# Attention denominators of 86 units: a DMA transpose and a VectorE reduction in place of matmuls with ones, with the PV matmuls ten slots behind

## The chip, the cores and the metric

The kernel runs on one core of one Trainium2 chip. The metric is the device time of one execution in microseconds; the time before is the median of three runs. The engines of the core are TensorE (PE in the profile), VectorE (DVE), ScalarE (ACT), GpSimd (POOL) and SyncE (SP), which issues nearly all DMAs of this kernel from one in-order queue.

## What is computed

An attention block over a given cache of keys and values (32 heads, 2048 queries, 2048 keys, head size 128) runs on a layer-normed input and is multiplied by a gate, the silu of a small mixer and MLP block. All data is bf16. The reference, cut to the attention:

```python
q = (xn @ wq).reshape(B, Sq, H, Dh).transpose(0, 2, 1, 3)
scores = jnp.einsum("bhqd,bhkd->bhqk", q, k_cache) * (Dh ** -0.5)
p = softmax(scores, axis=-1)
o = jnp.einsum("bhqk,bhkd->bhqd", p, v_cache)
s = o.transpose(0, 2, 1, 3).reshape(B, Sq, H * Dh) @ wo
g = silu(B_ref(xn, B_w1, B_w2, B_w3, B_w4))
out = x + s * g
```

The softmax is computed without subtracting a maximum: the exponentials of all 2048 keys are used as they are, and the sum over the keys, the denominator of a query, is applied to o.

## The kernel before

A first stage of some 120 us normalises the input and computes most of the gate branch. Then comes attention, in 128 units. A unit is one head and 512 queries. Heads go in eight groups of four (HG = 4); in a group the order is by block of queries and then by head, and the last group is arranged a little differently. With one head's 2048 keys on 16 chunks of 128, a unit has 8 slots (SPU = 8) of two chunks each. The main loop counts slots: n = 8u + p for slot p of unit u.

The program order of each engine is fixed by hand: every instruction goes through `pin`, which keeps it in the order written, and each engine works through its own list in order. One slot of the main loop writes, as far as they fall due:

- `s_slot(u, p)`: two matmuls of keys with q into a score bank pair `ps_s` (two such pairs), and one exponential on ACT into half of a tile `pT` (four tiles, so 8 slots' worth).
- `pv_slot` of slot n - LAG, with LAG = 5: two matmuls of values with exponentials into `ps_o`. There are two `ps_o` banks, one for each unit under way.
- slots 0 and 1: `q_mm`, four matmuls in all for the q of the next unit; slot 2: `q_copy` on DVE.
- slots 4 and 5: `wo_slot`, four matmuls of the output projection for 128 queries of an earlier block, and in slot 6 its DVE addition into `sacc`.
- denominators: DVE adds the unit's four `pT` tiles (`add_first` at slot 4, `add_next` at slot 6, `add_last` at slot 0 of the next unit). `add_last` also folds the sum to one row of 512 queries by 128 partitions, `acc[:, 0, :]`. At slot 3 of the next unit `sums` turns these 128 partial sums per query into one with four matmuls: a 128x128 block of `acc` as weights, a column of ones as the moving operand. DVE takes the reciprocal of the 128x4 result, and a DMA stores it in DRAM (`dr`). At slot 4 `bcast` reads it back to all partitions (`rb`, 128x512 f32).
- `norm(u)` at slot 2 of unit u + 2: DVE multiplies `ps_o` with `rb` into `oT`. That frees the `ps_o` bank, and after the last head of a group it makes a block ready for the projection.
- loads: in 9 of 16 units SP issues two pieces of a key tile, as DMA transposes, and half of a value tile for the next group; other units load wq and wo. There are five key tiles and five value tiles (HG + 1).

The last 20 units have a different end: some units run more projection tiles, and two of them compute their denominators in another way, which the change leaves as it is.

What the change touches: `sums` (lines 318 to 328), `bcast` and `rb` (330 to 333), `norm` (335 to 341), the tiles named `tm` in `wo_post`, `late_mul` and `late_act`, the `pT` tiles (line 288), and the main loop, lines 632 to 668.

Of the kernel before, what the change touches and what calls it, by code (L numbers as in the profile page):

```python
# [9 lines left out]
ALU = mybir.AluOpType  # L10
FP32 = mybir.dt.float32
BF16 = mybir.dt.bfloat16
# [5 lines left out]
def kernel(  # L18
# [15 lines left out]
    nc = tc.nc  # L34
    P = nc.NUM_PARTITIONS
# [3 lines left out]
    Sq, D = x2d.shape  # L39
# [11 lines left out]
    HG = 4  # L51
    NG = H // HG

    SPU = KC // 2
    LAG = 5
# [6 lines left out]
    pin = tc.keep_in_program_order  # L62
# [25 lines left out]
    smp = ent(pool("smp", 4))  # L88
    tokp = ent(pool("tok", 4))
    drp = ent(pool("drp", 4, bass.MemoryType.DRAM))  # L90
# [31 lines left out]
    units += [(NG - 1, qt, hh) for qt in range(QT - 2) for hh in range(HG)]  # L122
    units += [(NG - 1, qt, HG - 1) for qt in LATE]
    NU = len(units)
    NS = NU * SPU
    kTs, vBs, wqs, wos, oTs, st = {}, {}, {}, {}, {}, {}
    todo = defaultdict(list)
# [135 lines left out]
    def q_mm(u, dcs, tag="xa"):  # L263
        g, qt, hh = units[u]
        if dcs[0] == 0:
            st[u] = dict(psq=psX.tile([P, 512], FP32, tag=tag, name="ps_q"))
        for dc in dcs:
            mm(st[u]["psq"][:], wqs[g * HG + hh][:, dc, :],
               xnT[:, dc, qt * 512:(qt + 1) * 512], dc == 0, dc == DC - 1)
# [9 lines left out]
    def s_slot(u, p):  # L279
        g, qt, hh = units[u]  # L280
        s = st[u]
        sps = psS.tile([P, 2, 512], FP32, name="ps_s")
        for j in range(2):
            kc = 2 * p + j
            kv = kTs[g * HG + hh].rearrange("d (i p j) -> d i j p", p=P, j=KJ)
            mm(sps[:, j, :], kv[:, kc // KJ, kc % KJ, :], s["qT"][:], True, True)
        if p % 2 == 0:
            s.setdefault("pT", []).append(pB.tile([P, 4, 512], BF16, tag="pT", bufs=4, name="pT"))
        jj = 2 * (p % 2)
        pin(nc.scalar.activation(  # L290
            out=s["pT"][-1][:, jj:jj + 2, :], in_=sps[:], func=ACT.Exp, scale=SCALE))
# [11 lines left out]
    def add_last(u):  # L303
        add_next(u, 3)
        a = st[u]["acc"]
        pin(nc.vector.tensor_tensor(out=a[:, 0:2, :], in0=a[:, 0:2, :], in1=a[:, 2:4, :], op=ALU.add))  # L306
        pin(nc.vector.tensor_tensor(out=a[:, 0, :], in0=a[:, 0, :], in1=a[:, 1, :], op=ALU.add))  # L307

    def pv_slot(u, p):
        g, qt, hh = units[u]  # L310
        s = st[u]
        if p == 0:
            s["o"] = psO.tile([P, 512], FP32, tag="ps_o", name="ps_o")
        pT = s["pT"][p // 2]
        for j in range(2):
            kc = 2 * p + j
            mm(s["o"][:], vBs[g * HG + hh][:, kc, :], pT[:, 2 * (p % 2) + j, :], kc == 0, kc == KC - 1)

    def sums(u):
# [7 lines left out]
        s["dr"] = drp.tile([P, 4], FP32, name="dr")  # L327
        pin(nc.sync.dma_start(out=s["dr"][:], in_=rc[:]))

    def bcast(u):  # L330
        st[u]["rb"] = pB.tile([P, 512], FP32, tag="rb", bufs=5, name="rb")
        pin(nc.sync.dma_start(
            out=st[u]["rb"][:], in_=st[u]["dr"][:].rearrange("p j -> (p j)").partition_broadcast(P)))

    def norm(u):
        g, qt, hh = units[u]
        s = st.pop(u)
        if hh == 0:
            oTs[(g, qt)] = pB.tile([P, HG, 512], BF16, tag="oT", bufs=2, name="oT")
        pin(nc.vector.tensor_tensor(  # L340
            out=oTs[(g, qt)][:, hh, :], in0=s["o"][:], in1=s["rb"][:], op=ALU.mult))

    wo_box = {}
    sacc = {}
# [28 lines left out]
    def wo_post(g, t, n, eng=nc.vector):  # L373
        ps = wo_box.pop(0)
        if g == 0:
            sacc[t] = pS.tile([P, D], FP32, tag="sacc", bufs=NT, name="sacc")
            pin(nc.vector.tensor_copy(out=sacc[t][:], in_=ps[:]))
            return
        sa, gl = sacc[t][:], xall[:, t, :]
        if t // 4 in LATE and g >= GY:  # L380
            tm = pB.tile([P, D], FP32, tag="rb", bufs=5, name="tm")
            pin(nc.vector.scalar_tensor_tensor(
                out=tm[:], in0=ps[:], scalar=0.5, in1=gl, op0=ALU.mult, op1=ALU.mult))
            pin(nc.vector.tensor_tensor(out=sa, in0=sa, in1=tm[:], op=ALU.add))
            return
        pin(nc.vector.tensor_tensor(out=sa, in0=ps[:], in1=sa, op=ALU.add))  # L386
        if t // 4 in LATE and g == GY - 1:
            k = n + SPU * (t - 4 * LATE[0]) + 1
            at(max(k - SPU, n + 1), lambda: fin_load(t))
            at(k, lambda: y_scale(t))  # L390
            at(k + SPU, lambda: y_add(t))
        if g < NG - 1:
            return
        xl = fin.pop(t)
        pin(nc.vector.scalar_tensor_tensor(  # L395
            out=gl, in0=sa, scalar=0.5, in1=gl, op0=ALU.mult, op1=ALU.mult))
        pin(eng.tensor_tensor(out=xl[:], in0=gl, in1=xl[:], op=ALU.add))  # L397
        pin(nc.sync.dma_start(out=out2d[t * P:(t + 1) * P, :], in_=xl[:]))
# [30 lines left out]

    def late_mul(u, ts, ps):  # L430
        t = 4 * units[u][1] + ts
        tm = pB.tile([P, D], FP32, tag="rb", bufs=5, name="tm")
        pin(nc.vector.scalar_tensor_tensor(
            out=tm[:], in0=ps, scalar=st[u]["rc"][:, ts:ts + 1], in1=xall[:, t, :],
            op0=ALU.mult, op1=ALU.mult))
        return tm

    def late_act(u, ts, ps):
        t = 4 * units[u][1] + ts
        tm = pB.tile([P, D], FP32, tag="rb", bufs=5, name="tm")  # L440
        pin(nc.scalar.activation(out=tm[:], in_=ps, func=ACT.Identity, scale=st[u]["rc"][:, ts:ts + 1]))
        pin(nc.gpsimd.tensor_tensor(out=tm[:], in0=tm[:], in1=xall[:, t, :], op=ALU.mult))
        return tm
# [132 lines left out]
    pS = None  # L576
# [30 lines left out]
            at(n + 4, lambda: gate_silu(t, th["a"]))  # L607

    wo_todo = deque()

    def norm_queue(u):
        norm(u)
# [6 lines left out]

    UA, UB = NU - 2, NU - 1  # L620

# [9 lines left out]

    for n in range(UB * SPU):
        u, p = divmod(n, SPU)
        extra = u >= NU - 10 and len(wo_todo) > 1
        s_slot(u, p)
        m = n - LAG
        if 0 <= m < NS:
            pv_slot(*divmod(m, SPU))
        if p in (0, 1) and 4 * HG - 1 <= u:
            q_mm(u + 1, (2 * p, 2 * p + 1))  # L640
        if p == 0 and 1 <= u:
            add_last(u - 1)
        if p == 0:
            twice = extra
        if twice and p < 3:
            wo_slot(p, n)
        if p == 2 and 4 * HG - 1 <= u:
            q_copy(u + 1)
        late = u > NU - 4 * HG
        if p == 2 + late and 2 <= u:  # L650
            norm_queue(u - 2)
        if p == 3 + late and 1 <= u:
            sums(u - 1)
        if p == 4 + late and 1 <= u:
            bcast(u - 1)
        if p in (4, 5, 6) and wo_todo:
            wo_slot(p - 4, n)
        if p == 4:
            add_first(u)
        if p == 6:  # L660
            add_next(u, 2)
        held_mm(n)
        for fn in todo.pop(n, ()):
            fn()
        if not held and not todo.get(n + 1) and pS is None and n >= 4 * SPU + 5:
            right.close()
            pS = right.enter_context(pool("pS", side="right", reuse_waits="tile"))
# [14 lines left out]
    for p in range(SPU + LAG):  # L682
        if p < SPU:
            s_slot(UB, p)
        pv_slot(*divmod(UB * SPU + p - LAG, SPU))
        if p == 0:
            add_next(UA, 3)
        if p == 1:
            late_ps(UA)
            late_sums(UA, [st[UA]["acc"][:, i, :] for i in range(4)], True, True)  # L690
            late_rc(UA)
        if p == 2:
            norm_queue(UB - 2)
            for t in range(1, 4):
                fin_load(4 * (QT - 3) + t)
        if p in (3, 6, 8, 10):
            wo_tile(nc.gpsimd if p < 10 else nc.vector)
        if p == 4:
            late_o(UA, nc.vector)
            add_first(UB)  # L700
        if p == 5:
            late_tile(UA, 0, bank(psX, "xa"))
        if p in (5, 7, 9):
            late_tile(UA, (p - 3) // 2, bank(psO, "ps_o"))
        if p == 9:
            late_ps(UB)
            late_sums(UB, [st[UB]["acc"][:, i, :] for i in range(4)], True, False)
        if p == 10:
            late_sums(UB, [st[UB]["pT"][2][:, i, :] for i in range(4)], False, False)
        if p == 11:  # L710
            late_sums(UB, [st[UB]["pT"][3][:, i, :] for i in range(2)], False, False)
        if p == 12:
            late_o(UB, nc.scalar)
            late_sums(UB, [st[UB]["pT"][3][:, i, :] for i in range(2, 4)], False, True)
# [44 lines left out]
```

## Time and profile before

| | us |
|---|---|
| median of 3 runs | 1277.88 (1277.77 to 1278.06) |
| the profiled execution, its time | 1278.11 |
| the profiled execution, its span | 1276.3 |
| mean granted TensorE clock | 0.997 |

The span runs from the first to the last instruction of the profiled execution. In a row of a timeline the columns are start, duration, engine, source line, operation, output and inputs with their shapes, and how many instructions are merged in the row; in brackets stands the engine's idle time before the row and what ended it. Matmuls are pipelined: the next starts before the one before has ended, so durations of PE rows overlap, and the distance between starts tells the pace. All matmuls are recorded at the line of one helper, 107, so they are told apart by their tiles. A row of a DMA on SP shows for how long the issue held SP's queue; the time to landing, from issue until the data is there, is told by the DMA view.

### The profile page before, as it was taken

The numbers are of one execution on the slowest core, as the hardware profiler recorded it, in microseconds if no ns is written. First come the engines' busy times: TensorE is split into PE (matmuls) and PEld (weight loads), VectorE is DVE, ScalarE is ACT, GpSimd is POOL, SyncE is SP. The second block draws the span as 40 slices with busy tenths as digits, with TensorE's granted clock in tenths as the row PEclk, the third lists the DMA queues.
The fourth block names the chain that finished last, engine by engine and source line by source line (L and its number), as shares of the span: only waits on it lengthen the run. The fifth ranks groups of instructions, "written<-read, shape, count | busy, mean of one in ns | idle before, by whom it ended". The sixth has DMA issues, their size and how long they took to land.

```text
span 1276.3 us, 16933 instructions
## 1 busy us (share of the span) xinstructions
PE 1253.6 (98%) x6199; PEld 611.3 (48%) x6324; DVE 957.4 (75%) x1333; ACT 1056.4 (83%) x1108; POOL 46.5 (4%) x100
## 2 busy tenths in 40 slices
PE   8999999999999999999999999999999999999996
PEld 4444444444444444444444444444444444444443
DVE  7621567777777777777777777777778888888887
ACT  5444789988888888888888888888888888888884
POOL 4320000000000000000000000000000000000003
PEclk9999999999999999999999999999999999999998
DMA  8282012453133412453234303442235314351122
GB/s 207 54 161 59 9 26 50 83 100 63 38 80 71 98 34 50 92 87 55 50 74 85 83 28 74 84 83 50 55 71 112 71 42 91 71 95 34 26 67 75
DMA packets 170323, 90.52 MB, mean 71 GB/s; under 512 B 122432, under 2 KB 153664, under 8 KB 170240
## 3 DMA queue, kind: packets, MB, share of 16 engines
q1 hardware_dynamic: 166880, 86.55, 33.2%
q0 software_dynamic: 672, 1.84, 0.7%
q10 hardware_dynamic: 2688, 1.05, 0.3%
q8 instruction: 49, 0.80, 0.3%
q14 instruction: 34, 0.28, 0.1%
HBM read 67.11 MB, written 2.36 MB: 54 GB/s over the span
## 4 chain that ended last, share of the span: by engine, by line
PE 95%; ACT 2%; DVE 2%; issue 1%; DMA 0%; DVEq 0%; ACTq 0%
PE ps_s L107 38%; PE ps_o L107 37%; PE ps_wo L107 8%; PE ps_q L107 8%; PE ps_m L107 2%; PE ps_sum L107 1%; ACT pT L290 1%; DVE acc L301 0%; PE ps_warm L107 0%; DMA kT<-in_A_k_cache_dram 0%; ACT xnT L198 0%; DVE xall L395 0%; DVE sacc L386 0%; ACT qT L276 0%; DVE acc L306 0%
## 5 line engine op out<-in xcount | busy, mean ns | idle before, releaser
L290 ACT ACTIVATE pT<-ps_s 128x1024 bf16<-128x1024 f32 x1024 | 991.5, 1026 | 136.4 <-PE ps_s L107 130.2
L107 PE MATMUL ps_o<-pT,vb 128*128 128x512 bf16 x2023 | 604.2, 379 | 3.1
L107 PE MATMUL ps_s<-qT,kT 128*128 128x512 bf16 x1989 | 597.4, 380 | 3.7 <-ACT pT L290 1.2
L301 DVE TENSOR_TENSOR acc<-acc,pT 128x2048 bf16<-128x2048 bf16 x254 | 310.2, 1221 | 60.5 <-ACT pT L290 58.8
L107 PEld LDWEIGHTS <-kT 128*128 128x128 bf16 x2048 | 223.2, 114 | 206.0 <-issue 6.3
L107 PEld LDWEIGHTS <-vb 128*128 128x128 bf16 x2048 | 199.7, 98 | 225.2 <-issue 0.2
L296 DVE TENSOR_TENSOR acc<-pT 128x2048 bf16<-128x2048 bf16 x128 | 157.0, 1227 | 49.0 <-ACT pT L290 49.0
L107 PE MATMUL ps_wo<-wo_h,oT 128*128 128x512 bf16 x500 | 149.2, 379 | 0.1
L107 PE MATMUL ps_q<-xnT,wq_h 128*128 128x512 bf16 x485 | 142.8, 379 | 0.1
L386 DVE TENSOR_TENSOR sacc<-ps_wo,sacc 128x512 f32<-128x512 f32 x96 | 66.4, 691 | 69.4 <-PE ps_wo L107 69.4
L306 DVE TENSOR_TENSOR acc<-acc 128x1024 bf16<-128x1024 bf16 x126 | 87.1, 692 | 4.3
L340 DVE TENSOR_TENSOR oT<-ps_o,rb 128x512 bf16<-128x512 f32 x126 | 85.8, 681 | 0.7 <-DMA rb<-dr 0.7
L107 PEld LDWEIGHTS <-wq_h 128*128 128x128 bf16 x512 | 49.9, 98 | 59.7 <-issue 0.3
L274 DVE CAST qT<-ps_q 128x512 bf16<-128x512 f32 x112 | 76.6, 684 | 0.0
L107 PEld LDWEIGHTS <-oT 128*128 128x128 bf16 x504 | 48.4, 98 | 56.7
L307 DVE TENSOR_TENSOR acc<-acc 128x512 bf16<-128x512 bf16 x126 | 53.6, 426 | 4.3
L107 PEld LDWEIGHTS <-acc 128*128 128x128 bf16 x536 | 37.8, 114 | 29.3 <-DVE acc L301 0.7
L107 PE MATMUL ps_s<-xn2T,w_sb 128*128 128x512 bf16 x219 | 48.6, 380 | 0.3
L241 ACT ACTIVATE h2T<-ps_s 128x1024 bf16<-128x1024 f32 x28 | 28.6, 1023 | 24.1 <-PE ps_s L107 24.1
L397 POOL TENSOR_TENSOR xl<-xall,xl 128x512 bf16<-128x512 bf16 x3 | 3.4, 1148 | 1182.9 <-ACT pT L290 1182.9
L107 PEld LDWEIGHTS <-w_sb 128*128 128x128 bf16 x304 | 29.6, 98 | 34.8 <-issue 1.9
L326 DVE RECIPROCAL rc<-ps_sum 128x4 f32<-128x4 f32 x126 | 23.0, 183 | 27.4 <-PE ps_sum L107 14.3
(64 smaller groups left out, 382.9 us busy)
## 6 DMA issues: line engine op xcount, KB each, us to landing
rb<-dr SPq DMA_DIRECT2D x126, 256.0 KB, 4.2
vb<-in_A_v_cache_dram SPq DMA_DIRECT2D x64, 256.0 KB, 4.4
wo_h<-in_A_wo_dram SPq DMA_DIRECT2D x32, 128.0 KB, 4.2
wq_h<-in_A_wq_dram SPq DMA_DIRECT2D x28, 128.0 KB, 4.2
w_sb<-in_B_w_dram SPq DMA_DIRECT2D x9, 256.0 KB, 5.8
kT<-in_A_k_cache_dram SPq DMA_TRANSPOSE x128, 4.4
xl<-in_A_x_dram SPq DMA_DIRECT2D x16, 128.0 KB, 3.7
dr<-rc SPq DMA_DIRECT2D x126, 2.0 KB, 1.4
```

What stands on the lines that cost most here:

```text
L107: pin(nc.tensor.matmul(out=out, lhsT=lhsT, rhs=rhs, start=start, stop=stop))
L241: pin(nc.scalar.activation(out=h2[c, f][:], in_=ps[:], func=ACT.Gelu_apprx_tanh))
L274: pin(nc.vector.tensor_copy(out=qT[:], in_=st[u].pop("psq")[:]))
L290: pin(nc.scalar.activation(out=s["pT"][-1][:, jj:jj + 2, :], in_=sps[:], func=ACT.Exp, scale=SCALE))
L296: pin(nc.vector.tensor_tensor(out=s["acc"][:], in0=s["pT"][0][:], in1=s["pT"][1][:], op=ALU.add))
L301: pin(nc.vector.tensor_tensor(out=a[:], in0=a[:], in1=st[u]["pT"][i][:], op=ALU.add))
L306: pin(nc.vector.tensor_tensor(out=a[:, 0:2, :], in0=a[:, 0:2, :], in1=a[:, 2:4, :], op=ALU.add))
L307: pin(nc.vector.tensor_tensor(out=a[:, 0, :], in0=a[:, 0, :], in1=a[:, 1, :], op=ALU.add))
L326: pin(nc.vector.reciprocal(out=rc[:], in_=ps[:]))
L340: pin(nc.vector.tensor_tensor(out=oTs[(g, qt)][:, hh, :], in0=s["o"][:], in1=s["rb"][:], op=ALU.mult))
L386: pin(nc.vector.tensor_tensor(out=sa, in0=ps[:], in1=sa, op=ALU.add))
L397: pin(eng.tensor_tensor(out=xl[:], in0=gl, in1=xl[:], op=ALU.add))
```

## The change

It has four parts.

1. For the 86 units u = 22 to 107 (`TURN`) the four matmuls of `sums` go. In their place `turn(u)`, at slot 3 of unit u + 1, issues a DMA transpose of `acc[:, 0, :]` (128 x 512 bf16, SBUF to SBUF) into a new tile `tT` of 128 x 4 x 128. `turned_sums(u)`, at slot 0 of unit u + 2, reduces `tT` on DVE along its last dimension to 128x4, takes the reciprocal and issues the store to `dr`; it stands ahead of `add_last(u + 1)` on DVE. `bcast(u)` follows at slot 1 of u + 2, and `norm(u)` at slot 7 of u + 2, both later than before. The transposed order of the queries is made up for in `norm`, which reads `rb` with a step of four.
2. PV goes from five slots behind the scores to ten: `pv_run` raises the lag by one at each of units 18 to 22 (no PV in the first slot of these) and lowers it by one at each of units 111 to 115 (two PV slots in the first slot). In the program as built, DVE's list has `norm`, then the reduction, the reciprocal and the three adds of `add_last`; SP's list has, for each such unit, store, broadcast, transpose, and then the loads of keys and values.
3. `pT` gets six tiles instead of four, `rb` two instead of five; `tm` gets four tiles of its own.
4. In the last 20 units a second projection tile is computed in a unit as soon as more than three are waiting; before this began only in the last ten.

```diff
+    TURN = range(5 * HG + 2, NU - 5 * HG)
+    PV0, PV1 = 4 * HG + 2, NU - 5 * HG + 3
...
-            s.setdefault("pT", []).append(pB.tile([P, 4, 512], BF16, tag="pT", bufs=4, name="pT"))
+            s.setdefault("pT", []).append(pB.tile([P, 4, 512], BF16, tag="pT", bufs=6, name="pT"))
...
+    def turn(u):
+        st[u]["tT"] = pS.tile([P, 4, P], BF16, tag="tT", bufs=2, name="tT")
+        pin(nc.sync.dma_start_transpose(out=st[u]["tT"][:], in_=st[u]["acc"][:, 0, :]))
+
+    def turned_sums(u):
+        s = st[u]
+        sm = smp.tile([P, 4], FP32, name="sm")
+        pin(nc.vector.tensor_reduce(out=sm[:], in_=s["tT"][:], axis=mybir.AxisListType.X, op=ALU.add))
+        rc = smp.tile([P, 4], FP32, name="rc")
+        pin(nc.vector.reciprocal(out=rc[:], in_=sm[:]))
+        s["dr"] = drp.tile([P, 4], FP32, name="dr")
+        pin(nc.sync.dma_start(out=s["dr"][:], in_=rc[:]))
...
-        st[u]["rb"] = pB.tile([P, 512], FP32, tag="rb", bufs=5, name="rb")
+        st[u]["rb"] = pB.tile([P, 512], FP32, tag="rb", bufs=2, name="rb")
...
-        pin(nc.vector.tensor_tensor(
-            out=oTs[(g, qt)][:, hh, :], in0=s["o"][:], in1=s["rb"][:], op=ALU.mult))
+        o, rb, to = s["o"][:], s["rb"][:], oTs[(g, qt)][:, hh, :]
+        if u in TURN:
+            o, to = (x.rearrange("k (j p) -> k j p", j=4) for x in (o, to))
+            rb = rb.rearrange("k (p j) -> k j p", j=4)
+        pin(nc.vector.tensor_tensor(out=to, in0=o, in1=rb, op=ALU.mult))
...
+    pv_at = [0]
+
+    def pv_run(n):
+        u = n // SPU
+        if u < PV0:
+            lag = LAG
+        elif u < PV0 + LAG:
+            lag = LAG + u - PV0 + 1
+        elif u < PV1:
+            lag = 2 * LAG
+        else:
+            lag = max(LAG, 2 * LAG - (u - PV1 + 1))
+        while pv_at[0] <= min(n - lag, NS - 1):
+            pv_slot(*divmod(pv_at[0], SPU))
+            pv_at[0] += 1
...
-        extra = u >= NU - 10 and len(wo_todo) > 1
+        extra = len(wo_todo) > (1 if u >= NU - 10 else 3) and u >= NU - 5 * HG
         s_slot(u, p)
-        m = n - LAG
-        if 0 <= m < NS:
-            pv_slot(*divmod(m, SPU))
+        pv_run(n)
         if p in (0, 1) and 4 * HG - 1 <= u:
             q_mm(u + 1, (2 * p, 2 * p + 1))
+        if p == 0 and u - 2 in TURN:
+            turned_sums(u - 2)
+        if p == 1 and u - 2 in TURN:
+            bcast(u - 2)
         if p == 0 and 1 <= u:
             add_last(u - 1)
+        if p == 3 and u - 1 in TURN:
+            turn(u - 1)
...
-        if p == 2 + late and 2 <= u:
+        if p == (7 if u - 2 in TURN else 2 + late) and 2 <= u:
             norm_queue(u - 2)
-        if p == 3 + late and 1 <= u:
+        if p == 3 + late and 1 <= u and u - 1 not in TURN:
             sums(u - 1)
-        if p == 4 + late and 1 <= u:
+        if p == 4 + late and 1 <= u and u - 1 not in TURN:
             bcast(u - 1)
```

More of the change, by code (lines that the diff above doesn't have):

```diff
@@ L380, in wo_post @@
         if t // 4 in LATE and g >= GY:
-            tm = pB.tile([P, D], FP32, tag="rb", bufs=5, name="tm")
+            tm = pS.tile([P, D], FP32, tag="tm", bufs=4, name="tm")
             pin(nc.vector.scalar_tensor_tensor(
@@ L431, in late_mul @@
         t = 4 * units[u][1] + ts
-        tm = pB.tile([P, D], FP32, tag="rb", bufs=5, name="tm")
+        tm = pS.tile([P, D], FP32, tag="tm", bufs=4, name="tm")
         pin(nc.vector.scalar_tensor_tensor(
@@ L439, in late_act @@
         t = 4 * units[u][1] + ts
-        tm = pB.tile([P, D], FP32, tag="rb", bufs=5, name="tm")
+        tm = pS.tile([P, D], FP32, tag="tm", bufs=4, name="tm")
         pin(nc.scalar.activation(out=tm[:], in_=ps, func=ACT.Identity, scale=st[u]["rc"][:, ts:ts + 1]))
@@ L684 @@
             s_slot(UB, p)
-        pv_slot(*divmod(UB * SPU + p - LAG, SPU))
+        pv_run(UB * SPU + p)
         if p == 0:
```

## The prediction

> **What bounds the kernel now.** I read the page first: the span, the engines' shares, and the engine that makes up the chain of waits.
>
> ```profile
> span 1276.3 us, 16933 instructions
> PE 1253.6 (98%) x6199; PEld 611.3 (48%) x6324; DVE 957.4 (75%) x1333; ACT 1056.4 (83%) x1108; POOL 46.5 (4%) x100
> PE 95%; ACT 2%; DVE 2%; issue 1%; DMA 0%; DVEq 0%; ACTq 0%
> ```
>
> TensorE (PE) is busy throughout and makes 95% of the chain. A busy PE need not be at its peak, so next comes the timeline of PE in one attention unit in mid-kernel.
>
> ```profile
> 704.43 0.60 PE L107 MATMUL ps_s<-qT,kT 128*128 128x512 bf16 x2
> 704.86 0.60 PE L107 MATMUL ps_o<-pT,vb 128*128 128x512 bf16 x2
> ...
> 707.02 0.59 PE L107 MATMUL ps_s<-qT,kT 128*128 128x512 bf16 x2
> ...
> 708.32 0.59 PE L107 MATMUL ps_o<-pT,vb 128*128 128x512 bf16 x2
> 708.75 0.27 PE L107 MATMUL ps_sum<-ones_t,acc 128*128 128x1 bf16 x4
> 708.88 0.60 PE L107 MATMUL ps_s<-qT,kT 128*128 128x512 bf16 x2
> ...
> 717.51 0.27 PE L107 MATMUL ps_sum<-ones_t,acc 128*128 128x1 bf16 x4
> 717.64 0.60 PE L107 MATMUL ps_s<-qT,kT 128*128 128x512 bf16 x2
> ```
>
> Starts are what count. Two 512-column matmuls take 704.86 - 704.43 = 0.43 us; the four summing matmuls hold the next score matmul back by 708.88 - 708.75 = 0.13 us, and again by 717.64 - 717.51 = 0.13. One period is 717.64 - 708.88 = 8.76 us: 40 matmuls in 717.51 - 708.88 = 8.63, plus the sums' 0.13. No gap stands anywhere, so in this stage each matmul taken away shortens the unit, if nothing else becomes late. Slot 0 starts at 704.43, slots 0, 1, 4 and 5 hold six matmuls (1.29 us), the others four (0.86).
>
> **What the change removes.** TURN is range(22, 108), so 86 of the 126 summed units lose four weight loads and four matmuls.
>
> 86 x 0.13 us = 11.2 us, all on the path.
>
> The Trainium skill, "TensorE: Matmul & The Clock Gate", section LDWEIGHTS, gives a weight load as columns / 1.2 ns, some 107 ns for 128. If each load stood in the open, four would be 0.43 us a unit and the saving an estimated 37 us; the 0.13 us between starts says that they do not, and the row decides.
>
> **What it adds on VectorE (DVE).** A unit's work there now, with ScalarE (ACT):
>
> ```profile
> 703.34 2.86 ACT L290 ACTIVATE pT<-ps_s 128x1024 bf16<-128x1024 f32 x3 [0.27 <-PE ps_s L107]
> 706.36 1.02 ACT L290 ACTIVATE pT<-ps_s 128x1024 bf16<-128x1024 f32 x1 [0.17 <-PE ps_s L107]
> 707.71 2.85 ACT L290 ACTIVATE pT<-ps_s 128x1024 bf16<-128x1024 f32 x3 [0.33 <-PE ps_s L107]
> ...
> 705.31 1.23 DVE L301 TENSOR_TENSOR acc<-acc,pT 128x2048 bf16<-128x2048 bf16 x1 [0.58 <-ACT pT L290]
> 706.57 0.69 DVE L306 TENSOR_TENSOR acc<-acc 128x1024 bf16<-128x1024 bf16 x1
> 707.29 0.42 DVE L307 TENSOR_TENSOR acc<-acc 128x512 bf16<-128x512 bf16 x1
> 707.64 0.68 DVE L274 CAST qT<-ps_q 128x512 bf16<-128x512 f32 x1
> 708.24 0.68 DVE L340 TENSOR_TENSOR oT<-ps_o,rb 128x512 bf16<-128x512 f32 x1
> 709.05 0.18 DVE L326 RECIPROCAL rc<-ps_sum 128x4 f32<-128x4 f32 x1
> 709.68 1.23 DVE L296 TENSOR_TENSOR acc<-pT 128x2048 bf16<-128x2048 bf16 x1 [0.45 <-ACT pT L290]
> 711.67 0.69 DVE L386 TENSOR_TENSOR sacc<-ps_wo,sacc 128x512 f32<-128x512 f32 x1 [0.76 <-PE ps_wo L107]
> 712.28 1.22 DVE L301 TENSOR_TENSOR acc<-acc,pT 128x2048 bf16<-128x2048 bf16 x1
> ```
>
> These nine sum to 7.0 us of 8.76. The new reduction reads 512 bf16 elements a partition. Its bounds are the 0.42 us of the 512-element add and the 0.69 us of the 512-element f32 add; I take 0.65, near the upper, since four rows are summed one after another. The reciprocal stays at 0.18. DVE then has 7.7 us of 8.63: it fits, with 0.9 to spare. The product of line 340 now reads rb with a step of four floats, which no row shows; bounds 0.68 (unchanged) and 1.23 (the longest DVE instruction here), and I take 0.68, because its PSUM operand already holds it at the f32 add's pace. At 1.23 DVE still fits, at 8.2.
>
> A rule that speaks against this one: the Trainium skill, "SBUF — State Buffer", section Door 1, says that SBUF lines are 16 bytes and that an access which crosses to a new line pays. A step of four floats crosses at every element. It names no price; by the upper bound above DVE would still end inside the unit, so the sum stays and only the margin below shrinks by 0.55 us. No run so far shows it.
>
> **What it moves: the chain of a denominator.** After the change a unit's denominators travel: folded sum, DMA turn, reduction, reciprocal, store to DRAM (dr), broadcast (rb), product. DMA prices:
>
> ```profile
> rb<-dr SPq DMA_DIRECT2D x126, 256.0 KB, 4.2
> kT<-in_A_k_cache_dram SPq DMA_TRANSPOSE x128, 4.4
> dr<-rc SPq DMA_DIRECT2D x126, 2.0 KB, 1.4
> xn2T<-xn SPq DMA_TRANSPOSE x16, 2.4
> ...
> L332 SPq DMA_DIRECT2D rb<-dr x126: 319/320/339, 146.0 to 1248.0; - x126
> DMA to landing us min/median/max: 3.1/4.2/5.7
> ...
> L139 SPq DMA_TRANSPOSE kT<-in_A_k_cache_dram x128: 1127/1143/2904, 59.6 to 1143.6; - x128
> DMA to landing us min/median/max: 2.6/4.4/7.6
> ```
>
> The turn moves 128x512 bf16 from SBUF to SBUF as xn2T's transposes do (2.4 us from issue), but leaves just behind rb as kT's does now (4.4). Ends 2.4 and 4.4; I take 4.4 by its place in the queue, and keep kT's 7.6 for the range.
>
> On the clock of one unit (slot 0 at 0, period 8.63): the add of line 301 at slot 6 starts 712.28 - 704.43 = 7.85 after slot 0 and ends near 9.07; on the shorter grid the projection's addition ahead of it comes 0.13 earlier, so 8.95. The product waits its turn behind it: 8.95 to 9.6, which is 0.3 to 1.0 of the next unit. Then the reduction (to 1.6), the reciprocal (1.8), the last adds 1.23 + 0.69 + 0.42 (to 4.15). Store issued 1.85, landed 3.3; broadcast issued there, landed 7.5. Product due 8.95: 1.4 us in hand at the median, none at rb's slowest. The turn is issued at 4.15, landed 8.6; the reduction is due at 9.6: 1.0 us in hand. And a late product does not stop PE at once: its bank of ps_o is wanted by the PV matmuls of the unit two later, at slot 2, 8.63 + 2.59 + 0.43 = 11.65, two more microseconds. q's copy ends at 4.75 and is wanted at 8.63. So I cost the whole chain at nothing; what hides it is 8.63 us of PE work a unit, and the price when that is gone stands with the rivals.
>
> PV ten slots behind needs the exponentials longer: tile i of six is written again twelve slots later and its last PV goes out eleven slots after its first exponential, ahead of that slot's scores on the same in-order engine. No wait. The rb tile with two buffers is free at slot 7 of one unit and filled again near slot 3 of the unit after the next. Nothing either. Entering the lag drops a PV slot in each of five units, and one unit goes without output projection; both return later (double PV slots, an extra projection tile). In those units slots of 0.86 us meet exponentials that follow each other every (2.86 - 1.02) / 2 = 0.92 us: six short slots x 0.06, about 0.4 us lost. At the exit the first sums with ones stand at slot 3 (4.3) behind last adds that end at 4.15; a late product there costs up to 0.6 us in each of two units. I take nothing and keep 1.2 for the range.
>
> **Where ACT is close.** The score matmuls of slot 4 need the score buffer that slot 2's exponential frees. That one starts at 707.71 and ends 1.02 later, 708.73; without the sums slot 4 would start at 708.88 - 0.13 = 708.75. Slot 0 has the same margin today from the exponential of slot 6 (703.34 + 1.02 = 704.36 against 704.43, 0.07) and does not wait. With 0.02 instead of 0.07, the lost time is between 0 and 0.05 us a unit; I take a third of it, 0.017, since the margin is smaller than slot 0's but not below nothing: 1.5 us over 86 units.
>
> **The sum.** 11.2 - 0.4 - 1.5 = 9.3 us. The profiled execution took 1278.11 us (span 1276.3 and 1.8 around it); the median of the runs is 0.2 lower, 1277.88. 1277.9 - 9.3 = 1268.6 us.
>
> **SP's queue.** Each turn holds it 1.2 us, and each store waits for DVE ahead of everything behind.
>
> ```profile
> L232 SPq DMA_TRANSPOSE xn2T<-xn x16: 1189/1216/2505, 40.3 to 86.9; - x16
> ...
> 674.20 0.34 SPq L328 DMA_DIRECT2D dr<-rc  x1
> 675.61 0.34 SPq L332 DMA_DIRECT2D rb<-dr  x1
> 676.37 1.13 SPq L139 DMA_TRANSPOSE kT<-in_A_k_cache_dram  x1
> 677.61 0.51 SPq L149 DMA_DIRECT2D vb<-in_A_v_cache_dram  x1
> ...
> 586.00:595.00 9.00, 9.00 (x50) 4.50 (x49) 6.96 (x10) 7.99 (x10) 0.00 (x0) 1.00 0.16 31
> 560.00:569.00 9.00, 8.95 (x45) 4.39 (x45) 6.96 (x10) 7.99 (x9) 0.00 (x0) 1.00 0.57 90
> ```
>
> In a unit with K and V loads the queue issues dr 0.34, rb 0.34, turn 1.2, kT 1.13, vb 0.51, kT 1.13, 4.7 us of 8.63. The DMA share is 0.16 without and 0.57 with these loads; kT, vb and kT together add 0.41, so one more transpose some 0.14. It fits. The loads go out behind the turn, from 5.4 to 8.2, and the next store at 10.5.
>
> One load must wait: the V of a group's second head reuses the buffer of the first head, whose PV now ends five slots later, at slot 1 of the unit after (2.2 + 8.63 = 10.9), while the loads stand ready at 6.5. Today it leaves without a wait (the 0.51 above is this load). Behind it in the queue stand a kT, the store, the broadcast and the turn.
>
> **The rivals.**
>
> 1. That V load holds the queue. vb 10.9 to 11.5, kT to 12.6, the store 12.6 instead of 10.5, behind 384 KB: landed 14.6 to 15.4, rb 18.8 to 21.1, product ended by 19.5 to 21.8 against 20.3 wanted. PE loses 0 to 1.5 us directly, perhaps twice with the unit after, in groups 1 to 5: 0 to 15 us. At the middle, 7 us, the time is 1276. For it: the queue is in order. Against it: at the medians the product still ends in time.
>
> 2. ACT takes more. If slot 4 waits the full 0.05 us, 86 x 0.05 = 4.3 instead of 1.5, time 1271.4. For it: a margin of 0.02. Against: the two starts of slot 0 without a wait.
>
> 3. The turned sums become the period, the slower side. The ring on DVE is reduction 0.65, reciprocal 0.18, last adds 2.34, turn L, reduction: it fits 8.63 while L is under 5.46. Above that each 0.1 us costs 8.6 us, and from 5.6 on the change loses. With the turn landing in 5.7, rb's slowest, the loss is 0.24 x 86 = 21, the time 1268.6 + 21 = 1289; at kT's 7.6 it is 184, 1453. For it: kT at the same place reached 7.6. Against it: a median of 4.4 from DRAM, and 2.4 from SBUF. The ring over rb (product 0.68, reduction 0.65, reciprocal 0.18, dr 1.4, rb 4.2, 7.1 us) breaks only 1.5 us above its median; if rb slows by more, under the added transposes, this one sets the period in the same way, and its chance is counted here.
>
> The Trainium skill, "DMA: Bandwidth & Descriptors", section Latency and other measured facts, lets memory latency rise from 0.2 to 2 us under load. An estimate with that on rb would be 8.9 us for the last ring and 23 us lost over 86 units; rb's spread of 3.1 to 5.7 in this trace shows some of it, with DMA mostly idle.
>
> 4. Nothing gained: several small waits eat all of it, 1277.9.
>
> **How the numbers follow.** Forecast 0.60 (1265.9, with every cost but the 0.4 at nothing and 0.14 a unit saved, to 1270); ACT 0.10; V load 0.10; nothing 0.04; turned ring 0.16. A measurement of this kernel tells 0.2%, 2.6 us, from no change. Faster: 0.60 + 0.10 + half of the V load with a little of the rest, 0.77; same 0.06; slower 0.17. The range from 1265.5 to 1277 leaves out the slower tail and little else; the forecast's own range is 1265.9 to 1270.
>
> **What would show it.** No ps_sum matmuls between some 350 and 1070 us; PE starts 8.63 us apart from unit to unit; the reduction 0.65 and the product 0.68 us; turns landing in under 5 us; PE waiting for no oT. Wrong it would be if the list of waits shows PE ps_o waiting for oT, DVE sm waiting for tT by more than some 10 us, or a period over 8.70.

## The result, and the profile after

| | before | after |
|---|---|---|
| median, us | 1277.86 (1277.71 to 1278.06, 6 runs) | 1273.36 (1273.33 to 1273.58, 6 runs) |
| span of the profiled execution, us | 1276.3 | 1271.6 |
| mean granted TensorE clock | 0.997 | 0.997 |

The ratio is 0.9965, with a 95% interval of 0.9954 to 0.9976. The change gains 4.5 us, just under half of the 9.3 that were forecast (0.48 of it).

The head of the page after:

```profile
span 1271.6 us, 16361 instructions
PE 1245.2 (98%) x5862; PEld 600.4 (47%) x5980; DVE 1030.8 (81%) x1419; ACT 1056.6 (83%) x1108; POOL 46.7 (4%) x100
PE 91%; DVE 4%; ACT 3%; issue 1%; DMA 0%; POOL 0%; DVEq 0%; ACTq 0%
```

PE still makes up nearly all of the chain, with 337 of the recorded matmuls fewer, and DVE is busy for 73 us more. ACT and DVE have gained on the chain, and the two next views show where. First the PE timeline of one unit in mid-kernel (score matmuls only, the rows between them left out):

```profile
696.66 0.59 PE L107 MATMUL ps_s<-qT,kT 128*128 128x512 bf16 x2
...
697.96 0.59 PE L107 MATMUL ps_o<-pT,vb 128*128 128x512 bf16 x2
698.43 0.59 PE L107 MATMUL ps_s<-qT,kT 128*128 128x512 bf16 x2
...
701.02 0.59 PE L107 MATMUL ps_s<-qT,kT 128*128 128x512 bf16 x2
...
702.75 0.59 PE L107 MATMUL ps_s<-qT,kT 128*128 128x512 bf16 x2
...
707.10 0.59 PE L107 MATMUL ps_s<-qT,kT 128*128 128x512 bf16 x2
```

Slot 0 starts at 698.43 and again at 707.10, so a period is 8.67 us, not 8.63. The missing 0.04 us have one place: from 697.96 two matmuls last 0.43, which gives 698.39, and slot 0 starts at 698.43. From slot 6 to slot 0 it is 698.43 - 696.66 = 1.77 us, from slot 2 to slot 4, with just as many matmuls, 702.75 - 701.02 = 1.73. The list of waits does not have this stall at all: the rows of PE overlap by their modelled ends, and a gap of 0.04 us disappears under them. Only the distance between starts shows it. Slot 0 needs the score buffer that slot 6's exponential frees, so next comes ACT after:

```profile
692.98 2.85 ACT L292 ACTIVATE pT<-ps_s 128x1024 bf16<-128x1024 f32 x3 [0.27 <-PE ps_s L107]
696.00 1.02 ACT L292 ACTIVATE pT<-ps_s 128x1024 bf16<-128x1024 f32 x1 [0.17 <-PE ps_s L107]
697.36 4.02 ACT L292 ACTIVATE pT<-ps_s 128x1024 bf16<-128x1024 f32 x4 [0.33 <-PE ps_s L107]
```

Slot 6's exponential starts at 697.36 and ends 1.02 later, at 698.38; slot 0's matmuls follow at 698.43. Before, this exponential had 0.27 us of idle time ahead of it and that of slot 2 had 0.33 (703.34 and 707.71 in the prediction's rows). After, it is the other way round. The 0.06 us has moved by four slots.

The second place is at the end of the range that is turned. The list of PE's waits after, its first row, and two of its three places in PE's timeline (the third is 0.2 us, late in the kernel):

```profile
PE ps_sum L107 <- DVE qT L276: 2.4, 3, 1.4
```

```profile
1085.52 0.27 PE L107 MATMUL ps_sum<-ones_t,acc 128*128 128x1 bf16 x4 [1.35 <-DVE qT L276]
...
1096.16 0.27 PE L107 MATMUL ps_sum<-ones_t,acc 128*128 128x1 bf16 x4 [0.81 <-DVE qT L276]
```

These are the first ones-sums behind the turned range, those of units 108 and 109, which run in units 109 and 110. They wait for q's copy (line 276): `ps_sum` and `ps_q` share one PSUM bank, the tag xa, and DVE has not emptied it yet. Why not, its timeline after shows, from slot 6 of unit 108 on:

```profile
1078.95 1.22 DVE L303 TENSOR_TENSOR acc<-acc,pT 128x2048 bf16<-128x2048 bf16 x1
1080.09 1.08 DVE L359 TENSOR_TENSOR oT<-ps_o,rb 128x512 bf16<-128x512 f32 x1
1081.07 0.69 DVE L384 SCALAR_TENSOR_TENSOR sacc<-sacc,xall 128x512 f32<-128x512 f32 x1
1081.67 0.68 DVE L339 TENSOR_REDUCE sm<-tT 128x4 f32<-128x512 bf16 x1
...
1082.49 1.19 DVE L303 TENSOR_TENSOR acc<-acc,pT 128x2048 bf16<-128x2048 bf16 x1
...
1084.79 0.68 DVE L276 CAST qT<-ps_q 128x512 bf16<-128x512 f32 x1
```

DVE works without a break from 1078.95 to the copy's end near 1085.47, and PE's sums start at 1085.52. The product takes 1.07 us where it took 0.68, and a scaling of `sacc` stands in between. In unit 110 the two DVE instructions of an extra projection tile stand ahead of the copy, and it is late again.

To see how much each stretch gives, the distances between the starts of units (first weight load on a unit's keys) were added up from both traces, in us:

| units | before | after | difference | what it holds |
|---|---|---|---|---|
| start of unit 0 | 125.45 | 125.08 | -0.37 | not touched by the change |
| 0 to 4 | 59.96 | 60.02 | +0.06 | |
| 5 to 15 | 89.24 | 89.78 | +0.54 | not turned; 8.041 to 8.096 a unit |
| 16 to 22 | 61.37 | 59.87 | -1.50 | five PV slots left out, -2.16 |
| 23 to 106 | 736.40 | 727.57 | -8.83 | 8.767 to 8.670 a unit, -8.1; one projection less in unit 25, -0.7 |
| 107 to 112 | 52.60 | 56.54 | +3.94 | that projection and two PV slots, +1.72; the waits above, +2.16 |
| 113 to 126 | 123.63 | 124.85 | +1.22 | the other three PV slots, +1.29 |
| the rest | 27.7 | 27.9 | +0.2 | |

### The profile page after: what moved, and what is told of

It is laid out like the page before. It is cut to its first block, busy times and chain, and to the rows that moved or that the text cites. A ratio compares the mean times of both kernels' runs of the same rounds, so it can differ in the third digit from the quotient of the medians.

```text
span 1271.6 us, 16361 instructions
## 1 busy us (share of the span) xinstructions
PE 1245.2 (98%) x5862; PEld 600.4 (47%) x5980; DVE 1030.8 (81%) x1419; ACT 1056.6 (83%) x1108; POOL 46.7 (4%) x100
## 4 chain that ended last, share of the span: by engine, by line
PE 91%; DVE 4%; ACT 3%; issue 1%; DMA 0%; POOL 0%; DVEq 0%; ACTq 0%
PE ps_s L107 38%; PE ps_o L107 34%; PE ps_q L107 8%; PE ps_wo L107 8%; ACT pT L292 3%; PE ps_m L107 2%; DVE acc L303 1%; DVE xall L413 0%; PE ps_sum L107 0%; DVE sacc L404 0%; DVE tm L451 0%; ACT xnT L200 0%; DVE acc L308 0%; DMA xin<-in_A_x_dram 0%; DVE qT L276 0%
## 5 line engine op out<-in xcount | busy, mean ns | idle before, releaser
L107 PE MATMUL ps_s<-qT,kT 128*128 128x512 bf16 x2033 | 605.5, 379 | 4.4 <-ACT pT L292 1.2
L107 PE MATMUL ps_o<-pT,vb 128*128 128x512 bf16 x1963 | 589.7, 379 | 0.9
L107 PEld LDWEIGHTS <-kT 128*128 128x128 bf16 x2048 | 230.6, 114 | 229.0 <-issue 9.1
L107 PE MATMUL ps_q<-xnT,wq_h 128*128 128x512 bf16 x509 | 147.8, 379 | 1.2
L359 DVE TENSOR_TENSOR oT<-ps_o,rb 128x512 bf16<-128x512 f32 x126 | 119.7, 950 | 5.7 <-DMA rb<-dr 5.5
L339 DVE TENSOR_REDUCE sm<-tT 128x4 f32<-128x512 bf16 x86 | 58.7, 682 | 0.1
L107 PEld LDWEIGHTS <-h2T 128*128 128x128 bf16 x224 | 21.7, 98 | 26.7 <-issue 1.8
```

Source lines behind the costliest of these rows:

```text
L107: pin(nc.tensor.matmul(out=out, lhsT=lhsT, rhs=rhs, start=start, stop=stop))
L339: pin(nc.vector.tensor_reduce(out=sm[:], in_=s["tT"][:], axis=mybir.AxisListType.X, op=ALU.add))
L359: pin(nc.vector.tensor_tensor(out=to, in0=o, in1=rb, op=ALU.mult))
```

## The experiments

All are compared with the median after, 1273.36 us. The kernel before was run beside them at 1277.99.

In the program as built one exponential in each unit has its wait for the scores in a semaphore instruction of its own, followed by an exponential that waits only for ACT itself. It is the one whose `pT` tile was released by an add that another exponential has waited for already: `pT[0]` and `pT[1]` go free with one `add_first`. With four tiles that exponential stands at slot 2, with six at slot 6. The traces have it so: after, in unit 50, the semaphore instruction that waits for PE starts at 575.916 us and slot 6's exponential, which waits for ACT, at 575.977, 0.061 later. The theory, B, is that this form starts it 0.06 us later. Its rival A: with PV ten slots behind, the first weight load of a unit waits for q's copy (for VectorE), which before it did not. Rival C: two exponentials simply take longer than eight matmuls.

**One tile more.**

```diff
-    warm = const.tile([P, 512], BF16, name="warm")
+    warm = xall[:, NT - 1, :]
...
-tag="pT", bufs=6
+tag="pT", bufs=7
```

Here and with eight tiles, of a line that makes a tile only the arguments that differ are shown.

> Seven exponential tiles in place of six (the warm-up matmuls read a slice of xall, which is set to zero first, so that the 1 KB tile warm makes room); nothing else differs from the changed kernel. Theory B, the exponential whose wait on its scores stands in a separate semaphore instruction (gap before it 0.331 us against 0.272): it moves from slot 6 to slot 0, where the next scores that depend on it come 2.6 us later. Unit period 8.630 to 8.636 in place of 8.670, and units 7 to 15 go back by 0.055 each: 1273.36 - 86 x 0.035 - 0.7 = 1269.7 us (1269.2 to 1270.3). Theory A, the first weight load of a unit that waits for VectorE (q's copy): that wait is still there, so the period stays 8.67 and the time 1273.4 us, or 1272.7 with the early units alone. Theory C, the 0.035 is the exponential's own pace (two exponentials take longer than the PE's four matmul pairs whatever the wait): 1273.4 us.

Measured: 1268.97 us (1268.83 to 1270.56), 4.4 us faster. ACT and PE of this kernel, from slot 6 of one unit on:

```profile
690.97 2.86 ACT L292 ACTIVATE pT<-ps_s 128x1024 bf16<-128x1024 f32 x3 [0.27 <-PE ps_s L107]
```

```profile
690.34 0.60 PE L107 MATMUL ps_s<-qT,kT 128*128 128x512 bf16 x2
...
692.07 0.59 PE L107 MATMUL ps_s<-qT,kT 128*128 128x512 bf16 x2
...
700.70 0.60 PE L107 MATMUL ps_s<-qT,kT 128*128 128x512 bf16 x2
```

The idle time ahead of slot 6's exponential is 0.27 again, slot 6 to slot 0 is 1.73 us and a period 700.70 - 692.07 = 8.63. A and C fall. The gain is somewhat above the expectation because units outside the 86 have the same stall: 113 to 126 took 124.38 us in place of 124.85, and 16 to 22 59.50 in place of 59.87.

**The weight load's wait taken away.** q is computed and copied two units ahead.

```diff
-        if p in (0, 1) and 4 * HG - 1 <= u:
-            q_mm(u + 1, (2 * p, 2 * p + 1))
+        if p in (0, 1):
+            for w in qn:
+                q_mm(w, (2 * p, 2 * p + 1))
```

Here `qn` is u + 2 for units 24 to 105 and u + 1 around them; `q_copy` follows it.

> q's projection and its copy are made two units ahead instead of one for units 26 to 106 (one extra projection at unit 23, one left out at unit 106, so the amount of work is the same); six tiles as in the changed kernel. The first weight load of a steady unit then carries no wait on VectorE, and the exponential at slot 6 keeps its separate wait. Theory A: the 0.035 us at slot 0 go, 81 x 0.035 = 2.8, so 1270.5 us with a period of 8.635. Theory B and C: the period stays 8.67 and the time 1273.4 us (1273.0 to 1273.8).

Measured: 1273.86 us (1273.55 to 1275.46), units 8.670. In units 24 to 107 no first load waits for VectorE any more (the first four units of a group still wait for the DMA of their keys), and nothing is gained. The form of the wait on ACT, in its timeline, is as after:

```profile
698.25 4.02 ACT L293 ACTIVATE pT<-ps_s 128x1024 bf16<-128x1024 f32 x4 [0.33 <-PE ps_s L107]
```

A falls a second time.

**Six tiles alone, in the kernel before.** TURN is empty, PV stays five slots behind, and the extra projection tiles come as before. What is left of the change are the six tiles and, beside them, the rings that changed with them: `rb` with two tiles and `tm` with its own four.

```diff
-    TURN = range(5 * HG + 2, NU - 5 * HG)
-    PV0, PV1 = 4 * HG + 2, NU - 5 * HG + 3
+    TURN = range(0)
+    PV0 = NU
...
-            lag = max(LAG, 2 * LAG - (u - PV1 + 1))
+            lag = LAG
...
-        extra = len(wo_todo) > (1 if u >= NU - 10 else 3) and u >= NU - 5 * HG
+        extra = u >= NU - 10 and len(wo_todo) > 1
```

> The kernel before with one part of the change alone: six exponential tiles (two rb tiles, the products' tm tiles in their own ring); sums by matmuls, PV five slots behind, product at slot 2, all as before. Theory B: the separate wait moves from slot 2 to slot 6. Units 7 to 15, where ScalarE sets the pace, each get 0.055 us longer, 0.6 to 0.7 in all; in the units behind them slot 0 has the same eight matmuls in hand as in the changed kernel, so they too get 0.02 to 0.035 us longer, 90 to 110 of them: 1277.86 + 0.7 + 1.8 to 3.8 = 1280.4 to 1282.4 us; if the 0.13 us of the sums still cover it, 1278.5. Theory A: no weight load of a unit's start waits for VectorE here, so the late units stay at 8.767: 1277.9 to 1278.6 us. Theory C: 1277.9 us.

Measured: 1282.12 us (1282.05 to 1282.28), ratio to before 1.0031 (1.0019 to 1.0043). More exponential tiles without the turning make the kernel 4.1 us slower. Its units take 8.804 in place of 8.767, its units 5 to 15 89.81 us in place of 89.24. PE from slot 6 to slot 0, and ACT:

```profile
704.98 0.60 PE L107 MATMUL ps_s<-qT,kT 128*128 128x512 bf16 x2
...
706.75 0.59 PE L107 MATMUL ps_s<-qT,kT 128*128 128x512 bf16 x2
```

```profile
705.67 4.02 ACT L292 ACTIVATE pT<-ps_s 128x1024 bf16<-128x1024 f32 x4 [0.33 <-PE ps_s L107]
```

The stall is there, 1.77, without a turned sum, without the longer lag and without a first weight load that waits for VectorE, so A falls here too. It also explains units 5 to 15, where ACT is busy nearly all the time. Two rows of the early stage, before and then after:

```profile
232.84 6.52 ACT L290 ACTIVATE pT<-ps_s 128x1024 bf16<-128x1024 f32 x7 [0.27 <-PE ps_s L107]
```

```profile
232.87 6.52 ACT L292 ACTIVATE pT<-ps_s 128x1024 bf16<-128x1024 f32 x7 [0.33 <-PE ps_s L107]
```

Seven exponentials follow one another without a pause from slot 6 to slot 4. An exponential in the middle of such a run finds its scores ready, and its wait costs nothing whatever its form; that was slot 2. Slot 6 opens the run and does wait for PE, and there the form costs its 0.06 us a unit.

**Eight tiles.** If the place of the exponential is what counts, eight tiles bring it back to slot 2, and one more tile must lose again.

```diff
-tag="pT", bufs=6
+tag="pT", bufs=8
...
-tag="ta", bufs=10
+tag="ta", bufs=7
...
-tag="ou", bufs=2
+tag="ou", bufs=1
```

> Eight exponential tiles (room from the tile warm, three of the ten token tiles ta and one of the two tiles ou). Theory B: the exponential with the separate wait is now that of slot 2, and slot 4's scores, eight matmuls behind, wait for it as slot 0's did with six: period 8.65 to 8.67, units 7 to 15 at 8.04 as with seven tiles (there ScalarE is busy without a break at slot 2). 1268.97 + 0.02 to 0.037 x 100 = 1271.0 to 1272.7 us, so one tile more is slower than seven, if the smaller ring of token tiles costs nothing ahead of the units. Rival, the seventh tile helped as room, whatever the form of the wait: period 8.633 again and 1268.5 to 1269.2 us.

Measured: 1276.48 us (1275.33 to 1278.26). The units are as B had them: 8.670, and units 7 to 15 at 8.04. So the rival, which had 8.633, falls, and one tile more than seven loses what seven gained. The total is outside the expectation: unit 0 starts at 128.14 us, 3.1 later than after. 2.7 us of that are one wait of PE for the DMA of `xnT`, which after does not have; that the smaller rings, expected to cost nothing, are its cause was not tried. Three units (39, 71 and 103) are 0.28 us longer: in each the exponential of slot 2 has 0.61 us of idle time ahead of it in place of 0.33. Why stays open. ACT, and PE from slot 2 to slot 4:

```profile
695.55 4.02 ACT L292 ACTIVATE pT<-ps_s 128x1024 bf16<-128x1024 f32 x4 [0.33 <-PE ps_s L107]
```

```profile
694.86 0.59 PE L107 MATMUL ps_s<-qT,kT 128*128 128x512 bf16 x2
...
696.62 0.59 PE L107 MATMUL ps_s<-qT,kT 128*128 128x512 bf16 x2
```

The 0.33 stands at slot 2, and the stall, 1.76 us for eight matmuls, at slot 4. This is the stall that the prediction looked for at slot 4; where the tiles do bring it there, its size is 0.037 us a unit.

**The sums at the exit, two slots later.**

```diff
+        out2 = 2 * (u - 1 in (TURN.stop, TURN.stop + 1))
-        if p == 3 + late and 1 <= u and u - 1 not in TURN:
+        if p == 3 + late + out2 and 1 <= u and u - 1 not in TURN:
             sums(u - 1)
```

The broadcast and the product of these two units move by two slots as well.

> The ones-sums of units 108 and 109, the first two after the range that is turned, are put at slot 5 of the next unit instead of slot 3, their broadcast at slot 6 and their product two slots later. Theory E, the PE stall of 2.4 us in units 109 and 110 is these sums waiting for the PSUM bank that q's copy, late on VectorE, has to release: two slots are 2.2 us, so nearly all of it goes, 1273.36 - 2.2 = 1271.2 us (1270.9 to 1272.0), and units 109 and 110 last 8.9 to 9.7 us. Rival F, VectorE has more to do there than a unit is long, so the wait only passes to another tile (ps_wo, or the PV tile that waits for a product): less than 0.6 us, 1272.8 to 1273.4.

Measured: 1271.18 us (1271.0 to 1271.21), 2.18 faster; units 109 and 110 take 8.79 and 9.66 us in place of 10.10 and 10.64. Of the waits for qT only the late one of 0.2 us is left in PE's list, and no other has come in their place. The two sums in PE's timeline stand without idle time ahead of them:

```profile
1086.32 0.27 PE L107 MATMUL ps_sum<-ones_t,acc 128*128 128x1 bf16 x4
...
1095.97 0.27 PE L107 MATMUL ps_sum<-ones_t,acc 128*128 128x1 bf16 x4
```

E holds, F falls.

**The product in order.** The view of `rb` by steps of four is left out, so the queries get one another's denominators.

```diff
-        if u in TURN:
-            o, to = (x.rearrange("k (j p) -> k j p", j=4) for x in (o, to))
-            rb = rb.rearrange("k (p j) -> k j p", j=4)
```

> The product of the turned units reads and writes its 512 columns in order instead of by a step of 16 bytes (the queries of a tile then get one another's denominators, so the output is another one); six tiles, nothing else differs. If the step is what makes the product 1.07 us, it takes 0.68 again and VectorE has 0.39 us less per unit. Steady units do not wait for VectorE, so they stay at 8.670; at the exit q's copy in units 109 and 110 comes 0.39 us earlier each, so 1273.36 - 0.4 to 0.8 = 1272.6 to 1273.0 us. If VectorE's load had a part in the 0.035 us of each unit: 1269.7 to 1270.5 us. If the product's time has another cause (the PSUM tile, a late rb), it stays near 1.07.

Measured: 1272.58 us (1272.26 to 1273.0), units 8.670. The product's group, after (86 products with the step, 40 without) and in this kernel:

```profile
L359 DVE TENSOR_TENSOR oT<-ps_o,rb 128x512 bf16<-128x512 f32 x126 | 119.7, 950 | 5.7 <-DMA rb<-dr 5.5
```

```profile
L356 DVE TENSOR_TENSOR oT<-ps_o,rb 128x512 bf16<-128x512 f32 x126 | 86.1, 684 | 5.5 <-DMA rb<-dr 5.5
```

```profile
1085.12 0.27 PE L107 MATMUL ps_sum<-ones_t,acc 128*128 128x1 bf16 x4 [0.96 <-DVE qT L276]
...
1095.38 0.27 PE L107 MATMUL ps_sum<-ones_t,acc 128*128 128x1 bf16 x4 [0.43 <-DVE qT L276]
```

33.6 us less DVE work over 86 products, 0.39 each, and only 0.78 us of it reach the end, all at the exit: the two waits shrink from 1.35 and 0.81 to 0.96 and 0.43, by 0.39 and 0.38. The step and the view that makes it were left out together; a view of the same shape without a step was not tried. Inside the range DVE has room for the step.

The Trainium skill, "SBUF — State Buffer", section Door 1, says that an access that crosses to a new 16-byte line pays. The trace agrees: 1.07 us against 0.68 for the same 512 columns.

**Everything but the turning.** The calls of `turned_sums`, `turn` and the later `bcast` go, the sums by matmuls come back for all units, and the product is in order.

```diff
-        if p == 0 and u - 2 in TURN:
-            turned_sums(u - 2)
...
-        if p == 3 + late and 1 <= u and u - 1 not in TURN:
+        if p == 3 + late and 1 <= u:
```

> Everything of the change but the turning: PV ten slots behind, six exponential tiles, the product at slot 7 (in order), but the denominators of all units by matmuls with ones at slot 3 as before. Theory: the matmuls with ones cost their 0.134 us in each of the 86 units (8.804 against 8.670), 11.5 us, and VectorE, with neither reduction nor stepped product, no longer makes q's copy late at the exit: 1273.36 + 11.5 - 2.2 = 1282.7 us (1282.0 to 1283.4), about what six tiles alone gave (1282.12) with the ramps' 0.5 us. Rival: the stall at slot 0 and the sums' time cover one another, as the forecast for the kernel before had it (8.767): 1279 to 1280 us.

Measured: 1286.21 us (1285.36 to 1286.65), 3.5 above the expectation. Its units differ from those of the kernel with the later exit sums (1271.18) by 0.134 in units 26 to 34, as expected, which would make 11.5 us in 86. But from 36 to 94 they differ by 0.144 and in unit 35 by 0.45, for which no cause was looked for, in units 95 to 108 by 0.26 (unit 99 by 0.43), and in unit 110 by 0.58. DVE and PE in unit 100 show what was left out of the expectation for the units from 95 on:

```profile
1014.74 0.68 DVE L386 TENSOR_TENSOR sacc<-sacc,xl 128x512 f32<-128x512 f32 x1
...
1017.65 0.68 DVE L276 CAST qT<-ps_q 128x512 bf16<-128x512 f32 x1
```

```profile
1018.39 0.27 PE L107 MATMUL ps_sum<-ones_t,acc 128*128 128x1 bf16 x4
```

It is the exit's wait, in small. In these units DVE also scales and adds `sacc`; with the product at slot 7 these stand right ahead of the last adds, the copy ends at 1018.33, and the sums start only behind it. The expectation's rival, 1279 to 1280 us, falls: the stall at slot 0 and the sums' time add up. So the moves that make room for the turning (tiles, lag, late product) cost 1286.2 - 1278.0 = 8.2 us, and the turning takes 12.9 off again: 4.5 to 4.7 is what is left.

**Both repairs.** Seven tiles and the later exit sums.

> Seven exponential tiles and the later ones-sums of units 108 and 109 together. If the two costs are separate places, as theories B and E have it, the gains add: 1268.97 - 2.18 = 1266.8 us (1266.4 to 1267.1), with a unit period of 8.633 and units 109 and 110 at 8.8 and 9.6. If the faster units before bring a new wait at the exit (VectorE has 0.035 us less per unit), up to 0.5 us more: 1267.3.

Measured: 1266.86 us (1266.61 to 1268.45), ratio to before 0.9916 (0.9903 to 0.993). The two gains, 4.39 and 2.18, add up to 6.57; measured are 6.50. This version beats both kernels, before by 11.1 us.

## Why the prediction was wrong

The sign was right, and 1273.36 lies in its wide range (1265.5 to 1277), but the forecast of 1268.6 was 4.8 us too low, and the time is outside the forecast's own range (1265.9 to 1270). Two terms failed: the stall for ACT, taken as 1.5 us, cost 4.4, and the exit, taken at nothing, cost 2.2.

- *What the change removes.* Right: 0.134 us a unit, 11.5 us in 86, in place of 11.2.
- *The reduction.* Right: 0.68 us, taken 0.65.
- *The stepped product.* Taken 0.68, measured 1.07, inside the bounds. That DVE still fits was right for the steady units; at the exit it was 0.78 us of the loss. The reason given for 0.68, that the PSUM operand already sets the pace, did not hold.
- *The chain of a denominator at nothing.* Right. The turn's rows after:

```profile
L334 SPq DMA_TRANSPOSE tT<-acc x86: 1194/1219/2370, 338.4 to 1076.2; - x86
...
DMA to landing us min/median/max: 2.4/3.8/5.3
```

  It lands in 3.8 us at the median (4.4 taken), and at most in 5.3, under the 5.46 at which the ring on DVE would have become the period. PE never waited for `oT`, DVE never for `tT`. DVE waited 5.5 us in 8 products for `rb`, at most 1.0 in one, which reached no matmul. So the third rival fell; how far the ring is from breaking was not tried.
- *The ramp.* 0.4 us taken. With seven tiles, so without the stall at slot 0, units 16 to 22 lose 0.3 against five full PV slots (59.50 against 61.37 - 2.16), and the unit without a projection and its neighbour give 0.67 in place of the 0.86 of its four matmuls, 0.2 more. Nearly right: 0.5 in all.
- *Where ACT is close.* This is the step that failed. It looked at slot 4 and took 0.017 us a unit, 1.5 us, with 0.05 as the upper bound. The stall came at slot 0, 0.037 us in each unit from 16 on, so that the period became 8.67, above the forecast 8.63 and below the 8.70 that it named as its end, and 0.055 in units 7 to 15 in another way; the seventh tile shows the whole of it, 4.4 us. The prediction's own rows had the cause in view, 0.33 at slot 2 and 0.27 at slot 6, and treated them as belonging to the slots. They belong to the tile in the ring. Changing the ring from four to six moved them, and slot 0's 0.07 us in hand were 0.02 by the traces: 0.061 later made 0.037 of stall. The other 0.05 is what passes, even when PE stands waiting, from the end of the exponential to the matmul (698.38 to 698.43 after). So a margin read as end to start is 0.05 too large, and slot 4's 0.02 was already a lack of 0.03. "Slot 0 does not wait" was read from a program in which the longer wait was elsewhere.
- *The exit at nothing.* This failed as well: 2.18 us, above the 1.2 kept for the range. The prediction set the sums, at 4.3 of the unit's clock, against the last adds, which end at 4.15; what they wait for is q's copy, which the same clock had end at 4.75. It is the copy that comes behind the last adds on DVE and holds their PSUM bank, with the longer product and `sacc`'s instructions ahead of it.
- *The V load.* It did hold the queue, as the first rival had it. SP after, in such a unit, and its row in SP's list of waits:

```profile
669.40 1.25 SPq L141 DMA_TRANSPOSE kT<-in_A_k_cache_dram  x1
674.77 0.38 SPq L151 DMA_DIRECT2D vb<-in_A_v_cache_dram  x1
675.21 1.14 SPq L141 DMA_TRANSPOSE kT<-in_A_k_cache_dram  x1
676.44 0.53 SPq L343 DMA_DIRECT2D dr<-rc  x1
678.16 0.32 SPq L347 DMA_DIRECT2D rb<-dr  x1
```

```profile
SPq L151 <- PE ps_o L107: 18.9, 5, 4.1
```

  The load stood for some 4 us, and the store behind it came late. The product of that unit waited 0.78 us for `rb`, but these units take 8.670 like the others: the two microseconds that a product may be late covered it.
- *The second rival*, ACT's full 0.05 us a unit, 1271.4, was the nearest. Its 4.3 us are close to the 4.4 measured, but in part by luck: the stall is 0.037 a unit and not 0.05, it is at slot 0, and it reaches units outside the 86, which make up the difference.

The terms as measured: 11.5 less 4.4 for the wait's place, less 2.2 at the exit, less 0.5 at the ramp, is 4.4; the median fell by 4.5.

## What to carry to other kernels

Where a stage runs with hundredths of a microsecond in hand, the number of buffers in a ring is part of the schedule: it decides which instruction has the slower wait, so a change of it is to be costed at every slot, not only where the margin was smallest before, and one buffer more or less may be the cheapest repair. Beside the edge of a range that is treated in another way, follow each shared buffer to the engine that has to empty it, and add up that engine's list there, not in the steady state. When a small stall is looked for, compare distances between starts of equal pieces of work; a list of waits can miss it.

## What the hardware showed unexpectedly

- An exponential with its wait for PE in a separate semaphore instruction, followed by a wait for its own engine, had some 0.33 us of idle time ahead of it at slots 2 and 6 where the usual form had 0.27: in units 40 to 60 with four, six and eight tiles, and in units 7 to 15 with six, wherever ACT had to wait for its scores. Whether the separate instruction or the wait for its own engine costs the 0.06 us was not told apart.
- A product of 128x512 f32 with one operand in steps of 16 bytes took 1.07 us, in order 0.68.
- The pieces of keys landed sooner after the change, in 3.1 us at the median in place of 4.4, though SP's queue carries 86 transposes more. They no longer leave right behind the 256 KB of `rb`; that this is the reason was not tried.
